# Seven half-size products for batch one, and a new order of the pieces, in an attention and squared-ReLU kernel

## The chip, the core and the metric

The kernel runs on one core of a Trainium2 chip. Five engines run side by side, each through its own queue in order: TensorE (PE, matmuls, with the weight loads shown as PEld), VectorE (DVE), ScalarE (ACT), GpSimd (POOL) and SyncE (SP, which here only issues DMAs). They wait for one another on semaphores. The metric is the time of one execution in device microseconds; the time before is 215.47 us, the median of 3 runs from 215.01 to 215.59.

## What is computed

Two steps, joined. In the first, for each of 8 batches and 8 heads, 512 rows of `x` (64 wide) attend to 32 state rows, and the 32 state rows attend to the 512 rows of `x`:

```python
a = softmax(scale * x @ state.T);   xread = a @ state     # 512 rows
a2 = softmax(scale * state @ x.T);  sread = a2 @ x        # 32 rows
attn_out = concatenate([xread, sread], axis=2)
```

The heads are laid side by side, which gives 8 * 544 = 4352 tokens of width 512. In the second step each token goes through two layers, 512 to 2048 and back to 512:

```python
h = tokens @ w_in
r = maximum(h, 0)
g = s * (r * r) + b
out = g @ w_out
```

## The kernel before

A program writes the instructions from a list of short words, `ORDER` (lines 15 to 78). Each word is one piece of work, its numbers are the batch and the part, and a last letter, where there is one, is the engine: A for ACT, V for DVE, G for POOL. The loop at lines 736 to 739 reads the list from front to back and calls the function of each word from the table `pieces`. Since every engine works through its own queue in order, the list sets, for each engine, the order of its pieces; what is written for different engines runs side by side as far as the semaphores let it.

One batch passes through these pieces.

- Attention of the 512 rows: `x` loads the batch (POOL issues two DMAs; from batch 3 on behind a tiny copy, `ahead`, that waits for the transpose `xT` of the batch before), `xT` transposes it (DVE), `T` makes the scores (PE), `U` transposes them, `mu`, `D`, `E1`, `z`, `At` and `A` are the softmax in between (DVE, E1 on ACT, `D` and `At` on DVE or POOL). `A` is what the first layer multiplies.
- Because the attention is linear in the states, `M` (PE) multiplies the states with `w_in`, 512 columns at a time (four pieces), and `Mc` copies the result from PSUM into f16 (ACT or DVE).
- First layer: `l.b.f` (line 483) multiplies A and M for 128 of the 2048 columns, two matmuls of 512 columns, into `hps`, and ACT takes the ReLU into `r`. `hps` has two PSUM buffers. Batch 0 does part of it in halves of 256 tokens (`lh`). `s` squares two or four such blocks into `g` (`sh` for halves), on ACT or DVE.
- Second layer of batches 0 and 1: `L.b.rr.q` (line 510), four matmuls of 512 columns that sum a quarter of the 2048 for 128 tokens, and `out`, which scales, adds the bias and stores (DVE, then DMAs from SP).
- Second layer of batches 2 to 7: seven products of half-size blocks in place of eight (a Strassen-like scheme). `g` and `w_out` are cut into 2 x 2 blocks. `wsum` makes the sums T1 to T4 of the weight blocks once (eight DVE pieces). `S.b.k.h` makes the four sums of the activation blocks, two halves each (1024 columns a half), mostly in place. `P.b.u` (line 596), u from 0 to 13, is half of one of the seven products: eight matmuls of 256 columns into one of three PSUM tiles, X, Y and W, which share two buffers. `ev` (line 611) scales and adds them into the output tile, seven evictions on DVE, and `put` stores.
- Attention of the 32 state rows: `nm`, `nms`, `E2`, `a2` are the softmax, `tr` transposes by DMA, `xn` loads `x` in another layout (four POOL DMAs; two buffers), `V` (PE, line 408) multiplies, `srd` (ACT) collects. At the end `lsr`, `ssr`, `S_sr`, `P_sr` and `ev_sr` take all 256 of these rows through the two layers.

Three kinds of PE pieces use small tiles of the array, 64 or 128 rows by 32 or 64 columns: `T`, `M` and `V`, and with them `cps` (column sums of `w_out`, for the bias). They write to one of two pairs of PSUM banks, made by `two_banks` (line 133): pair "pt" when `own` is 1, pair "pa" when it is 0. A third number on `M` and `T` chooses; `V` always took "pa". A piece can write to its pair when the piece before it there has been copied out.

POOL's queue carries the loads of `x`, `xn`, `w_in` and `w_out` in the order of the list, and the few pieces marked G in between. SP's queue carries the stores and `tr`.

Of the kernel before, what the change touches and what calls it, by code (L numbers as in the profile page):

```python
# [77 lines left out]
]  # L78


# [1 line left out]
def kernel(  # L82
# [17 lines left out]
    B, H, S, D = x.shape  # L100
# [3 lines left out]
    P = 128  # L104
# [28 lines left out]
    def two_banks(name, dtype=FP32, own=False):  # L133

        pool, tag = (ps_t, "pt") if own else (ps_a, "pa")
        return pool.tile([P, 2, 2048 // mybir.dt.size(dtype)], dtype, name=name, tag=tag)
# [27 lines left out]
    own = konst.tile([P, 2], FP32, name="own")  # L164
# [240 lines left out]
        a2T = sm(b, "a2T", [P, NG * SCH, P], FP16, apool, 2)  # L405
        nc.sync.dma_start_transpose(out=a2T, in_=at[b]["a2"].rearrange("p g s -> p (g s)"))

    def at_V(*bs):

        pair = two_banks(f"vps_{bs[0]}")  # L410
        for v, b in enumerate(bs):
            vps = pair[:, v, : NK * Ns].rearrange("p (k n) -> p k n", n=Ns)
            a2T, xn = at[b]["a2T"], xn_t[b]
            for k in range(NK):
                for g in range(NG):
                    hp = k ^ 2 * g
                    for i in range(SCH):
                        mm(
                            vps[D * g : D * g + D, k, :],
                            xn[:, 4 * g + k, i, :],  # L420
                            a2T[:, SCH * g + i, Ns * hp : Ns * hp + Ns],
                            start=(i == 0),
                            stop=(i == SCH - 1),
                            tp=(0, D * g),
                        )
            at[b]["vps"] = vps
# [343 lines left out]
```

## Time and profile before

The profiled execution took 214.72 us; its span, from the first to the last instruction, is 212.9 us. It ran with a mean granted TensorE clock of 0.989.

| what | us | count |
|---|---|---|
| first layer, matmuls `hps`, busy | 66.1 | 240 |
| second layer of batches 0 and 1, matmuls `ops`, busy | 31.9 | 128 |
| ReLU `r` on ACT, busy | 69.2 | 120 |
| loads `xn` on POOL | 18.6 | 32 |
| chain that ended last: share of PE | 77% | |

"Busy" counts the time in which at least one instruction of the group ran, so overlapping instructions count once. The "mean" of a group is the length of one instruction from start to end; where instructions overlap, the next one starts before that. In a view in order of time a row gives the start, the length of a merged run, the engine, the line, what is written and read, the shape, and how many instructions were merged. In brackets stands the idle time before it and what ended it. Most matmuls of this kernel carry the line of a helper, 140, so they are told apart by the tile that they write: `opf_X`, `opf_Y`, `opf_W` are the products P, `ops` the pieces L, `hps` the pieces l, `mps` the pieces M, `vps` the pieces V, `T_None` the pieces T.

### The profile page before, as it was taken

The numbers are of one execution on the slowest core, as the hardware profiler recorded it, in microseconds if no ns is written. First come the engines' busy times: TensorE is split into PE (matmuls) and PEld (weight loads), VectorE is DVE, ScalarE is ACT, GpSimd is POOL, SyncE is SP. The second block draws the span as 40 slices with busy tenths as digits, with TensorE's granted clock in tenths as the row PEclk, the third lists the DMA queues.
The fourth block names the chain that finished last, engine by engine and source line by source line (L and its number), as shares of the span: only waits on it lengthen the run. The fifth ranks groups of instructions, "written<-read, shape, count | busy, mean of one in ns | idle before, by whom it ended". The sixth has DMA issues, their size and how long they took to land.

```text
span 212.9 us, 4690 instructions
## 1 busy us (share of the span) xinstructions
PE 202.8 (95%) x1891; PEld 126.6 (59%) x1891; DVE 179.5 (84%) x272; ACT 170.9 (80%) x279; POOL 42.8 (20%) x72
## 2 busy tenths in 40 slices
PE   7688999999999999999999999999999999999991
PEld 2224443344444447667777567677675778888881
DVE  2899999999999979899999899989799563766671
ACT  4589988899979899989999989999698998454300
POOL 8554002771202130002404007006200000000000
PEclk9979999999999999999999999999999999999998
DMA  6999999199950939306961881628932640070045
GB/s 148 178 206 207 195 205 166 12 150 226 184 125 4 147 62 161 75 4 129 191 129 22 130 198 17 85 49 150 204 46 49 154 97 3 17 183 0 2 127 173
DMA packets 32107, 24.54 MB, mean 115 GB/s; under 512 B 12884, under 2 KB 25940, under 8 KB 32084
## 3 DMA queue, kind: packets, MB, share of 16 engines
q0 software_dynamic: 16848, 12.52, 41.0%
q1 hardware_dynamic: 13952, 10.75, 21.0%
q10 hardware_dynamic: 1284, 0.95, 1.5%
q8 instruction: 15, 0.25, 0.4%
q14 instruction: 8, 0.07, 0.1%
HBM read 25.72 MB, written 8.91 MB: 163 GB/s over the span
## 4 chain that ended last, share of the span: by engine, by line
PE 77%; DVE 9%; ACT 7%; DMA 3%; issue 1%; SPq 1%; DVEq 0%
PE hps L466 21%; PE opf_X L140 17%; PE ops L515 13%; PE opf_W L140 7%; PE opf_Y L140 4%; PE hps_sr L466 3%; ACT g L474 3%; PE mps L140 3%; DMA out_dram<-osx 3%; PE dps L684 2%; PE ops_sr_X L140 2%; PE T_None L140 2%; DVE Dm L335 1%; DVE g L476 1%; ACT r L470 1%; PE vps L140 1%
## 5 line engine op out<-in xcount | busy, mean ns | idle before, releaser
L470 ACT ACTIVATE r<-hps 128x512 f16<-128x512 f32 x120 | 69.2, 614 | 11.8 <-PE hps L466 11.0
L466 PE MATMUL hps<-A,M 128*128 128x512 f16 x240 | 66.1, 380 | 0.3 <-ACT rh L496 0.2
L140 PEld LDWEIGHTS <-g 128*128 128x128 f16 x576 | 55.9, 98 | 16.7 <-issue 1.5
L474 ACT ACTIVATE g<-r 128x1024 f16<-128x1024 f16 (+1 forms) x36 | 42.8, 1210 | 0.2
L466 PEld LDWEIGHTS <-M 128*128 128x128 f16 x240 | 22.2, 98 | 18.9 <-issue 5.4
L515 PE MATMUL ops<-w_out,g 128*128 128x512 f16 x128 | 31.9, 379 | 0.0
L585 DVE TENSOR_TENSOR g<-g 128x1024 f16<-128x1024 f16 (+1 forms) x34 | 24.3, 715 | 3.2 <-PE opf_Y L140 1.8
L196 POOL DMA_DIRECT2D xn<-in_x_dram x32 | 18.6, 601 | 38.9 <-PE vps L140 37.4
L155 ACT CAST M<-mps 128x1024 f16<-128x1024 f32 x25 | 25.7, 1035 | 0.9 <-PE mps L140 0.9
L140 PE MATMUL opf_X<-w_T,g 128*128 128x256 f16 x192 | 24.6, 273 | 0.2 <-DVE osx L615 0.2
L515 PEld LDWEIGHTS <-g 128*128 128x128 f16 x128 | 12.2, 98 | 15.1 <-DVE Dm L335 0.4
L615 DVE SCALAR_TENSOR_TENSOR osx<-opf_X,sb_bc,bias_bc 128x512 f32<-128x512 f32 x18 | 13.4, 743 | 6.7 <-PE opf_X L140 5.5
L476 DVE TENSOR_TENSOR g<-r 128x1024 f16<-128x1024 f16 (+1 forms) x14 | 11.6, 830 | 3.1 <-ACT r L470 2.9
L140 PE MATMUL mps<-w_in,stT 64*32 64x512 f16 x256 | 12.5, 407 | 1.2 <-DMA w_in<-in_moe_w_in_dram 1.0
L470 ACT ACTIVATE r_sr<-hps_sr 128x256 f16<-128x256 f32 x16 | 6.1, 383 | 9.0 <-PE hps_sr L466 8.7
L140 PE MATMUL opf_Y<-w_out,g 128*128 128x256 f16 x96 | 12.5, 273 | 0.0
L140 PE MATMUL opf_X<-w_out,g 128*128 128x256 f16 x96 | 12.3, 273 | 0.0
L140 PE MATMUL opf_W<-w_out,g 128*128 128x256 f16 x96 | 12.3, 273 | 0.0
L140 PE MATMUL opf_X<-w_T,S 128*128 128x256 f16 x96 | 12.0, 273 | 0.0
L140 PE MATMUL opf_W<-w_T,g 128*128 128x256 f16 x96 | 11.8, 273 | 0.0
L184 POOL COPY ahead<-xT 1x2 f16<-1x2 f16 x5 | 2.5, 507 | 42.6 <-DVE xT L301 42.6
L140 PEld LDWEIGHTS <-S 128*128 128x128 f16 x96 | 9.3, 98 | 2.6 <-issue 0.4
(95 smaller groups left out, 284.0 us busy)
## 6 DMA issues: line engine op xcount, KB each, us to landing
out_dram<-osx SPq DMA_DIRECT2D x44, 128.0 KB, 2.4
xn<-in_x_dram POOLq DMA_DIRECT2D x32, 128.0 KB, 5.1
xh<-in_x_dram POOLq DMA_DIRECT2D x14, 256.0 KB, 4.6
w_in<-in_moe_w_in_dram POOLq DMA_DIRECT2D x8, 256.0 KB, 9.2
w_out<-in_moe_w_out_dram POOLq DMA_DIRECT2D x4, 512.0 KB, 13.9
out_dram<-osb SPq DMA_DIRECT2D x16, 64.0 KB, 5.2
out_dram<-osb SPq DMA_DIRECT2D x8, 128.0 KB, 3.3
xf<-in_x_dram SPq DMA_DIRECT2D x2, 256.0 KB, 3.6
```

The lines of the kernel that those rows point to most:

```text
L140: return nc.tensor.matmul(out, lhsT, rhs, start=start, stop=stop, tile_position=tp, is_transpose=is_transpose, skip_group_check=skip,)
L155: (engine.copy if engine is nc.scalar else engine.tensor_copy)(out, in_)
L184: nc.gpsimd.tensor_copy(ahead, at[b - 1]["xT"][0:1, 0, 0])
L196: nc.gpsimd.dma_start(out=xn_t[b][32 * jh : 32 * jh + 32].rearrange("t h c d -> t h (c d)"), in_=x[b].rearrange("h (t jh c) d -> jh t h (c ...
L466: nc.tensor.matmul(hps, lhsT, rhs, start=(i == 0), stop=(i == len(terms) - 1))
L470: nc.scalar.activation(R_t[tag, q][:, i], hps, AF.Relu)
L474: nc.scalar.activation(g, r, AF.Square)
L476: e.tensor_mul(g, r, r)
L515: nc.tensor.matmul(ops_t[tag, rr], G_t[tag][:, f, P * rr : P * rr + P], w_out_f(f), start=(v == 1 and f == 4 * q), stop=(v == NKF // 4 and ...
L585: e.tensor_tensor(out, x, y, op)
L615: nc.vector.scalar_tensor_tensor(out, fast(b, name[0]), s_bc, out if plus else bias, ALU.mult, ALU.add)
L684: nc.tensor.matmul(dps, ones16[:, :P], ones16, start=True, stop=True)
```

## The change

Three things change in the code. `V` gets a number in front that chooses the PSUM pair. In the list, batch one's second layer is no longer 16 pieces L with four `out`, but 14 pieces P with eight S, seven `ev` and four `put`. And from the word `sb` on the list stands in a new order, in which some pieces also change engine or PSUM pair. In front of `sb` nothing changes.

```diff
-    def at_V(*bs):
+    def at_V(own, *bs):
 
-        pair = two_banks(f"vps_{bs[0]}")
+        pair = two_banks(f"vps_{bs[0]}", own=own)
```

The list past `sb` before (its first part, which has the head, and the part in which batch one's second layer begins):

```diff
-    "lh.0.0.0 sh.0.0.0.V lh.0.6.0 sh.0.6.0.V lh.0.2.1 xT.1.1 sh.0.2.1.V wout.2 sb lh.0.0.1 M.0.2.0 T.1.1 "
-    "U.1 Mc.0.2.A lh.0.4.0 lh.0.4.1 mu.1 D.1.V sh.0.4.0.A l.0.10 keep.1 L.0.1.0 lh.0.6.1 sh.0.6.1.V "
-    "l.0.11 M.1.2.1 l.0.9 M.0.3.0 E1.1 l.0.8 s.0.10.2.V Mc.0.3.V",
...
-    "s.1.8.2.V cps.3 l.1.15 mu.2 c L.0.1.3 L.0.0.3 keep.2 x.3 l.1.7 l.1.12 M.2.1.1 Mc.2.1.A xT.3 "
-    "sh.0.4.1.A bias D.2.G l.1.13 out.0.1 L.0.0.2 T.3.1 nm.3 U.3 E1.2 M.2.2.0 l.1.5 sh.0.0.1.A nms.3.A "
...
-    "s.1.6.2.A L.0.3.0 L.1.0.2 s.1.4.2.A M.3.0.0 M.2.3.1 l.2.0 l.1.14 wsum.T2.0.V L.1.0.1 wsum.T4.0.V "
```

and after:

```diff
+    "lh.0.0.0 sh.0.0.0.V lh.0.6.0 sh.0.6.0.V lh.0.2.1 xT.1.1 sh.0.2.1.V wout.2 sb lh.0.4.0 lh.0.4.1 "
+    "M.0.2.0 sh.0.4.0.V Mc.0.2.A T.1.1 U.1 lh.0.0.1 lh.0.6.1 M.1.2.0 mu.1 sh.0.4.1.G l.0.9 keep.1 l.0.8 "
+    "D.1.V E1.1 L.0.0.0 l.0.11 Mc.1.2.V L.0.1.0 z.1 At.1.V",
+    "M.0.3.1 M.1.3.0 Mc.0.3.A l.0.10 A.1 l.0.12 l.0.15 L.0.0.1 s.0.10.2.V Mc.1.3.A l.0.13 pair.4.16 l.1.9 "
+    "L.0.1.1 turn.4.12.V s.0.12.2.A l.0.14 l.1.15 xT.2 M.2.0.0 l.1.10 l.1.11 wsum.T1.0.V T.2.1 keep.2 "
+    "l.1.8 l.1.1 s.0.8.2.G L.0.0.2 Mc.2.0.V s.0.14.2.V U.2 wsum.T3.0.V l.1.3 wout.3 x.3 xn.2 sh.0.0.1.A "
+    "l.1.0 xn.3 cps.0 cps.2 s.1.8.2.A cps.1 cps.3 M.2.1.1 L.0.1.2 s.1.10.2.A mu.2 L.0.1.3 wsum.T1.1.V "
+    "Mc.2.1.A l.1.7 c l.1.2 D.2.G E1.2 xT.3 bias L.0.0.3 l.1.6 out.0.1 l.1.13 s.1.0.4.V out.0.0 T.3.1 "
+    "M.2.2.0 l.1.12 s.1.6.2.A wsum.T2.0.V L.0.2.3 x.4 l.1.14 l.1.5 sh.0.6.1.A s.1.12.4.A z.2 L.0.2.2 U.3 "
+    "L.0.3.3 Mc.2.2.A L.0.3.2 At.2.G L.0.3.1",
+    "nm.3 nms.3.A E2.3.1 wsum.T3.1.V l.1.4 mu.3 A.2 L.0.2.0 E2.3.0 L.0.2.1 l.2.7 xT.4 out.0.2 l.2.5 "
+    "s.1.4.2.A M.2.3.0 wsum.T2.1.V T.4.1 l.2.8 wsum.T4.1.V l.2.2 L.0.3.0 a2.3 Mc.2.3.A D.3.G l.2.1 "
+    "out.0.3 l.2.10 E1.3 P.1.1 S.1.3.1.V U.4 nm.4 S.1.1.1.G l.2.0 S.1.3.0.G l.2.4 nms.4.A P.1.3 E2.4.0 "
+    "E2.4.1 x.5 turn.12.16.A tr.3 mu.4 P.1.0 l.2.6 l.2.3 P.1.2 M.3.0.1 M.3.1.0 ev.1.X1 s.2.4.2.A "
+    "S.1.2.1.V l.2.13 s.2.6.2.V ev.1.Y S.1.1.0.V P.1.5 Mc.3.1.A s.2.2.2.A P.1.7 S.1.2.0.V l.2.15 "
+    "s.2.0.2.A z.3 P.1.4 l.2.9 At.3.V l.2.11 ev.1.X2 xn.4 Mc.3.0.A D.4.V V.0.3 P.1.6 srd.3 l.2.14 l.2.12 "
+    "A.3 S.1.4.0.V P.1.9 M.4.2.0 M.3.2.1",
...
+    "Mc.6.0.A s.5.2.2.A l.5.6 M.6.1.1 M.6.2.0 s.5.12.2.G l.5.0 P.4.4 E2.0.0 l.5.4 l.5.1 put.3.1.0 P.4.6 "
...
+    "S.5.1.1.V l.6.4 put.4.0.0 S.5.2.0.G s.6.14.2.A ev.5.X1 S.5.2.1.V l.6.9 P.5.5 ev.5.Y P.5.4 l.6.5 "
```

Counted over the whole list, pieces change engine like this: three more `Mc` on ACT and three fewer on DVE; of the squares `s`, eleven instead of fourteen on DVE, 37 instead of 36 on ACT, two on POOL; one half square `sh` from ACT to POOL; on POOL also `D.3`, `S.1.1.1`, `S.1.3.0`, `S.5.2.0`, and `At.2` in place of `At.6`.

93 rows, old and new, of the table ORDER are left out of this document.

## The prediction

> **What bounds the kernel now.** I read the page's totals first, then the busy time by stretches, then the chain of waits, and last the order of time around single steps. The totals and the time slices:
>
> ```profile
> span 212.9 us, 4690 instructions
> PE 202.8 (95%) x1891; PEld 126.6 (59%) x1891; DVE 179.5 (84%) x272; ACT 170.9 (80%) x279; POOL 42.8 (20%) x72
> PE   7688999999999999999999999999999999999991
> ```
>
> TensorE (PE) has no visible hole between the fourth slice (about 21 us) and the last. A busy PE can still run below its peak, so I looked at what full pieces cost in the chain of waits, and at the stretches:
>
> ```profile
> 44.99 2.59 PE ops L515 x12
> 87.46 1.75 PE opf_W L140 x16
> 189.68 0.87 PE opf_Y L140 x8
> ```
>
> ```profile
> 20.00:100.00 80.00, 79.58 (x634) 39.19 (x633) 76.44 (x101) 74.18 (x118) 17.44 (x29) 1.00 0.75 124
> 100.00:120.00 20.00, 19.88 (x257) 14.29 (x256) 18.76 (x28) 19.16 (x31) 4.64 (x8) 1.00 0.72 120
> ```
>
> The columns are the stretch, its length, then busy time of PE, weight loads, VectorE (DVE), ScalarE (ACT), GpSimd (POOL), the granted clock, and DMA. Twelve matmuls of 512 columns pass in 2.59 us, sixteen of 256 columns in 1.75 us, at a granted clock of 1.00: each costs what its columns cost, and pieces of one kind cost the same early and late. So from 20 us on a microsecond of PE work removed is a microsecond saved, as long as nobody is late for PE. The two helpers are nearly full too: between 20 and 100 us DVE is idle for 80 - 76.4 = 3.6 us and ACT for 5.8 us. That is the margin in which this change has to live.
>
> **PE's saving.** A piece L (four matmuls of 512 columns) costs 2.59 / 3 = 0.863 us, a piece P (eight of 256) 1.75 / 2 = 0.874. Batch one gives up 16 L, 13.81 us, and gets 14 P, 12.23 us: 1.58 us saved. The second saving is in the small tiles, the pieces M, T, V and cps:
>
> ```profile
> 38.09 1.03 PE L466 MATMUL hps<-A,M 128*128 128x512 f16 x4
> 39.05 0.41 PE L140 MATMUL mps<-w_in,stT 64*32 64x512 f16 x8
> 39.39 0.39 PE L140 MATMUL bps<-c,ones 128*128 128x512 f16 x1
> 49.67 0.62 PE L140 MATMUL mps<-w_in,stT 64*32 64x512 f16 x16
> 50.23 1.04 PE L466 MATMUL hps<-A,M 128*128 128x512 f16 x4
> ```
>
> Two l pieces cost half of 1.73 us (eight such matmuls), 0.86, yet they take 39.05 - 38.09 = 0.96 before a small piece, which then holds PE for 0.34: a lone M costs 0.44. Two M side by side hold it for 50.23 - 49.67 = 0.56, with the same 0.10 in front 0.66, so the second adds 0.22. Each pair of groups merged saves 0.2 us. In the old order the 51 small pieces stand in 29 groups, in the new one in 26: 0.6 us. PE's floor falls by 1.58 + 0.6 = 2.2 us. The weight loads have room (39 of 80 us busy). Nothing else changes on PE.
>
> **What the other engines get.** Their prices:
>
> ```profile
> L474 ACT ACTIVATE g<-r 128x1024 f16<-128x1024 f16 x30 | 31.2, 1058 | 0.1
> L474 ACT ACTIVATE g<-r 128x2048 f16<-128x2048 f16 x6 | 11.8, 1972 | 0.1
> L474 ACT ACTIVATE g<-rh 128x512 f16<-128x512 f16 x3 | 1.9, 649 | 0.0
> L155 ACT CAST M<-mps 128x1024 f16<-128x1024 f32 x25 | 25.7, 1035 | 0.9 <-PE mps L140 0.9
> L155 DVE CAST M<-mps 128x1024 f16<-128x1024 f32 x7 | 8.5, 1216 | 0.8 <-PE mps L140 0.8
> L585 DVE TENSOR_TENSOR g<-g 128x1024 f16<-128x1024 f16 x32 | 21.9, 683 | 1.4 <-PE opf_X L140 1.0
> L615 DVE SCALAR_TENSOR_TENSOR osx<-opf_X,sb_bc,bias_bc 128x512 f32<-128x512 f32 x18 | 13.4, 743 | 6.7 <-PE opf_X L140 5.5
> L525 DVE SCALAR_TENSOR_TENSOR osb<-ops,sb_bc,bias_bc 128x512 f32<-128x512 f32 x8 | 5.9, 734 | 0.0
> L335 POOL TENSOR_TENSOR Dm<-U,mu 128x1024 f32<-128x1024 f32 x1 | 1.9, 1908 | 4.9 <-DVE mu L331 4.9
> L356 POOL TENSOR_TENSOR At<-E,rz 128x1024 f16<-128x1024 f16 x1 | 1.9, 1909 | 11.9 <-DVE rz L347 11.9
> ```
>
> DVE over the whole kernel: six sums S of batch one at 0.68 and seven evictions at 0.74 come (+9.3); four stores at 0.73, three casts Mc at 1.22, D.3 (priced as a cast) and S.5.2.0 go (-8.5); its squares become two fewer of the two-wide and one fewer of the four-wide kind (-2.6, a square taken as a sum of its width). Net -1.8 us. ACT: three casts at 1.03, one four-wide square at 1.97, one half square of 0.65 fewer: +4.4 us. POOL gets six more whole operations at 1.9 (D.3, S.1.1.1, S.1.3.0, S.5.2.0, s.0.8.2, s.5.12.2), one half (sh.0.4.1, about 1.0), and trades At.6 for At.2: +12.4 us, in a queue that idles 80%. No row shows POOL squaring or adding f16 sums; the two rows of POOL arithmetic are 1.91 for f32 and f16 alike, so I take 1.9; the bounds are DVE's 0.68 for the same sum and 2.6, should it wait out one such sum first.
>
> What matters is where it falls. Up to the first product of batch three (about 99 us), counting list against list, ACT has one cast more, one two-wide and one four-wide square more, one half square less: +1.03 + 1.04 + 1.97 - 0.65 = +3.4 us. The stretch gets shorter by most of PE's saving, say 1.8. ACT's idle time there falls from 5.8 to 5.8 - 3.4 - 1.8 = 0.6 us: ACT becomes as full as PE. DVE's load there falls by about 1.3, its idle time ends near 3.6 + 1.3 - 1.8 = 3.1.
>
> One ACT wait I can name. E1.2 now stands behind D.2 on POOL, and D.2 behind ten loads (x.3, xn.2, xn.3) where it had only x.3:
>
> ```profile
> 32.16 0.55 POOL L184 COPY ahead<-xT 1x2 f16<-1x2 f16 x1 [10.83 <-DVE xT L301]
> 38.61 1.91 POOL L335 TENSOR_TENSOR Dm<-U,mu 128x1024 f32<-128x1024 f32 x1 [4.87 <-DVE mu L331]
> 40.85 1.11 POOL L187 DMA_DIRECT2D xh<-in_x_dram  x2 [0.20 <-issue]
> 46.80 0.58 POOL L196 DMA_DIRECT2D xn<-in_x_dram  x1 [0.78 <-DMA xh<-in_x_dram]
> 41.59 1.08 ACT L341 ACTIVATE E<-Dm 128x1024 f16<-128x1024 f32 x1
> ```
>
> Ten such loads in one go took from 40.85 to 47.38, 6.5 us. Started when x.3 starts now, or up to 1 us earlier because xT.2 moves up, they end at 38.2 to 39.2, and D.2 at 40.1 to 41.1 instead of 40.52. ACT, however, comes to E1.2 sooner: the same 18 first-layer, 7 L and 4 half pieces stand in front of it that PE has done by 39.05 (row above), so with the last relu about 39.6, where it now comes at 41.59. Behind E1.2 queue the relus of l.1.6 and l.1.13, and PE has two PSUM buffers for them; then it waits. ACT's forced idle is 0.5 to 1.5 us.
>
> wout.3, the last quarter of w_out, is moved behind a POOL square whose relus come from the first l pieces, so to about 26 us instead of 20.58:
>
> ```profile
> 20.58 0.75 POOL L210 DMA_DIRECT2D w_out<-in_moe_w_out_dram  x1 [1.79 <-DMA w_out<-in_moe_w_out_dram]
> DMA to landing us min/median/max: 11.2/13.9/14.6
> xh<-in_x_dram POOLq DMA_DIRECT2D x14, 256.0 KB, 4.6
> ```
>
> cps.2, cps.3 and the first L of that quarter need it near 36 us. With 13.9 it would land at 39.9 and PE lose up to 4; with twice the 4.6 us of a load of half its size that meets a shorter queue, at 35.2, and nothing is lost. The landing times grow from 11.2 to 14.6 us because each waits for the loads ahead; after 21.3 POOL issues none until 32.16, so a later issue mostly finds the queue shorter. I take nothing, near the second row. The early xn loads follow it and are needed only by V, far later.
>
> The sums of the weights (T1 to T4) move ahead of batch one's products and number eight as before. The V pieces may take either PSUM pair: no instruction is added. The tail (the last sums and stores) has the same pieces; nothing there, since PE's last products cover the sums; if one came late, its 0.7 would be the price.
>
> **The loss.** Bounds on what ACT's fullness costs PE: at the low end nothing; at the high end all of the 5.8 us idle stays, because it was waiting for data, and PE loses 5.8 - 0.6 = 5.2. The nearest row is the stretch from 100 to 120, with ACT 96% busy, in which one PE wait stands:
>
> ```profile
> 119.47 0.41 PE L140 MATMUL mps<-w_in,stT 64*32 64x512 f16 x8
> 120.05 0.41 PE L140 MATMUL mps<-w_in,stT 64*32 64x512 f16 x8 [0.17 <-ACT M L155]
> ```
>
> 0.58 instead of 0.22: 0.36 us in 20, or 1.4 in 80. I take half of that, 0.7, which is also the lower half of the E1.2 wait, because the rest of ACT's idle time is time in which it was ahead of PE.
>
> Sum: -2.2 + 0.7 = -1.5 us. The profiled execution, 214.72 us with 212.9 of span, would become 213.2. It lies 0.75 under the median of the runs shown (215.47), so for the median I say 215.47 - 1.5 = 214.0.
>
> **Rivals.** *ACT becomes the bound* (the slower side). Place: ACT's queue from the head to batch three. If 4 of its 5.8 us idle are true waits, PE loses 4 - 0.6 = 3.4 and the time is 215.47 - 2.2 + 3.4 = 216.7. It decides from 3.5 us of idle that stays (loss 2.9, gain gone). For it: every square moved to ACT. Against it stands the largest of ACT's waits, for PE's hps (view of waits: total, times, longest): there ACT was ahead of PE.
>
> ```profile
> ACT r L470 <- PE hps L466: 11.0, 23, 1.0
> ```
>
> *A draw*: 1.6 to 2.8 us lost, about 215.2. *All of it arrives*, or the head's waits shrink too: 213.3 and below; the lists part at sb, 17.4 us, where PE still waits.
>
> *DVE and POOL hold each other up.* Beside today's two POOL operations DVE ran none with two SBUF tensors:
>
> ```profile
> 129.04 1.91 POOL L356 TENSOR_TENSOR At<-E,rz 128x1024 f16<-128x1024 f16 x1 [11.86 <-DVE rz L347]
> 129.37 1.24 DVE L327 STREAM_TRANSPOSE U<-T_None 128x1024 f32<-128x1024 f32 x1
> 131.16 0.68 DVE L585 TENSOR_TENSOR g<-g 128x1024 f16<-128x1024 f16 x1
> ```
>
> So its trace cannot say whether a sum on DVE would have waited. With seven more, each can hold a DVE sum for up to its 1.9 us. The new order puts transposes, reductions and evictions beside most of them (U.4, nm.4, mu.4 and an eviction, 4.4 us, beside the two sums of batch one, 3.8), but ev.5.X1 alone, 0.74, stands beside S.5.2.0, so a wait of 1.2 is in sight there. If half of all 12.4 us block DVE, 6.2 less the 3.1 idle: 3.1 lost, 215.47 - 1.5 + 3.1 = 217.1. The Trainium skill (SBUF — State Buffer, Who interferes with whom) states just this: a DVE instruction with two SBUF inputs and a GpSimd one that reads SBUF exclude each other for a whole instruction. No run here shows it yet.
>
> *It does not do what it says*: the products of batch one could wait for the weight sums. All of T1 to T4 stand in the list ahead of the product that reads them, so I give that nothing.
>
> **Chances.** Forecast 0.42 (faster); all of it arrives 0.16 (faster); draw 0.20; ACT the bound 0.14; DVE and POOL 0.08. Faster 0.58, same 0.20, slower 0.22, where 0.3%, 0.65 us, is what a measurement here can tell from no change. The forecast's own range is 213.3 to 214.8. For 8 in 10 it must take in the draw and the nearer part of the slower cases: 212.8 to 216.7.
>
> **What would show it.** Right: x112 more opf matmuls, 64 fewer ops; PE's last piece about 1.5 us earlier; ACT busy about 77 of the first 78 us after 20; E1.2 waiting for Dm on POOL about 1 us. ACT the bound: PE waits with ACT as releaser between 40 and 90 us. DVE and POOL: sums on DVE longer than 0.68 while POOL computes, or POOL rows longer than 1.9. Wrong altogether: PE waits named for osx, S or x loads in batch one's products.

## The result, and the profile after

The changed kernel takes 213.65 us, the median of 9 runs (212.66 to 214.59), against 215.59 us (215.01 to 216.5, 9 runs) before: a ratio of 0.9907, 95% interval 0.9881 to 0.9934. A second set of runs gave 0.9923 (0.9895 to 0.995). The profiled execution took 212.66 us, 2.06 less than the one before. Its page:

```profile
span 210.9 us, 4809 instructions
PE 200.8 (95%) x1939; PEld 131.3 (62%) x1939; DVE 178.0 (84%) x273; ACT 175.2 (83%) x282; POOL 56.1 (27%) x79
PE 66%; ACT 16%; DVE 10%; DMA 3%; issue 1%; SPq 1%; DVEq 0%
L517 PE MATMUL ops<-w_out,g 128*128 128x512 f16 x64 | 15.6, 379 | 0.0
```

PE has 48 instructions more (112 more of the products, 64 fewer of `ops`), as announced, and is busy 2.0 us less. The third line is the chain of waits: it runs 16% of the span through ACT, where it was 7%. The last rows of the chain before and after, which hold PE's last piece:

```profile
207.58 0.89 PE ops_sr_X L140 x8
```

```profile
205.89 0.89 PE ops_sr_X L142 x8
```

PE's last piece comes 1.69 us earlier. Of the 1.97 us by which the span is shorter, the other 0.28 lies behind this piece, in the last eviction and store. The busy time by stretches, columns as before:

```profile
20.00:100.00 80.00, 79.39 (x732) 44.63 (x730) 78.31 (x105) 78.41 (x123) 29.92 (x38) 1.00 0.73 123
100.00:120.00 20.00, 19.59 (x214) 13.98 (x212) 19.26 (x30) 19.14 (x31) 0.71 (x2) 1.00 0.59 121
```

ACT, the fourth busy time, is now idle for 1.6 of 80 us and DVE, the third, for 1.7, while PE still loses only 0.6. The chain from the first of these rows to the last:

```profile
42.80 0.60 ACT r L472
...
70.94 1.83 ACT M L157 x2
72.81 0.37 PE mps L142
```

Between them every piece of the chain is one of ACT's, although PE has no hole there before the last row. Both are full, and the tracing back takes ACT. This is the state that the prediction called "as full as PE".

To see where PE lost time I priced every piece of its list with the prediction's prices (0.863 an L, 0.874 a P, 0.43 an l, 0.22 an M or cps and 0.22 more for each group of small pieces; T and V at what they take in the trace), summed from `sb` on, and compared each piece's start with this sum. What a piece is late by is what PE has waited so far. The sum falls by 2.2 us, as forecast, and the waits grow by 0.5. A new one of 0.57 stands at the piece P.3.5, a product of batch three; the rest about cancels (0.25 for one of ACT's casts at 72.8 us is new, 0.26 at 120 us and 0.22 at P.5.5 are gone). The order of time around it:

```profile
103.44 0.75 DVE L617 SCALAR_TENSOR_TENSOR osx<-opf_X,sb_bc,bias_bc 128x512 f32<-128x512 f32 x1 [0.56 <-DMA out_dram<-osx]
104.25 1.03 PE L142 MATMUL opf_X<-w_T,g 128*128 128x256 f16 x8 [0.41 <-DVE osx L617]
```

and the chain of waits that leads to it:

```profile
95.11 0.67 DVE osx L617
...
97.05 0.59 SPq L626
...
97.68 5.64 DMA out_dram<-osx
...
103.44 0.76 DVE osx L617
...
104.25 1.03 PE opf_X L142 x8
```

The last eviction of batch two into its first output tile, ev.2.W2, ends at 95.77. SP then issues eight stores one after the other, 0.6 us each, the four of this tile first; the chain follows the fourth, issued at 97.68, whose transfer ends at 103.32. This tile (key 0) holds the first half of the batch's rows, with all columns; the expectations below that call it the tile of columns 0 mean the same one. It has one buffer, so batch three's first eviction, ev.3.X1, waits 0.56 us for the store, and P.3.5, which adds to the PSUM tile that this eviction reads, waits for it. In the kernel before, the same eviction stood at 104.71 and waited for nothing:

```profile
95.18 0.74 DVE L615 SCALAR_TENSOR_TENSOR osx<-opf_W,sb_bc,osx 128x512 f32<-128x512 f32 x1
...
104.71 0.71 DVE L615 SCALAR_TENSOR_TENSOR osx<-opf_X,sb_bc,bias_bc 128x512 f32<-128x512 f32 x1
```

There it was 9.5 us from the start of the one to the start of the other. In the new order it would have been 7.9 (95.03 to 102.88, where DVE began to wait), and the way through the store takes 8.4 (95.03 to 103.44).

The shorter distance alone would not have met the store. Before, the four stores of this tile landed 2.3 to 2.4 us after their issue, the fourth 5.0 us after the start of ev.2.W2; now they take 5.1 to 5.7. What differs beside them is POOL's load `x.7`, two transfers of 256 KB: it is now issued just ahead of the stores, where before it came when the first of them had landed. The rows before, in order of time, with the stores issued between 94 and 101 us (KB each, us to landing):

```profile
95.95 7.85 SPq L624 DMA_DIRECT2D out_dram<-osx  x8
98.76 1.05 POOL L187 DMA_DIRECT2D xh<-in_x_dram  x2 [0.31 <-issue]
...
out_dram<-osx SPq DMA_DIRECT2D x4, 128.0 KB, 2.3
```

and after:

```profile
95.10 1.06 POOL L189 DMA_DIRECT2D xh<-in_x_dram  x2
95.80 5.17 SPq L626 DMA_DIRECT2D out_dram<-osx  x8
```

That the load lengthens the stores is read from the traces side by side (before, the batch's later stores, issued at 101.9 to 103.2 beside POOL's loads, took 4.9 to 5.4 us too). No run moves the load alone.

### The profile page after: what moved, and what is told of

It is laid out like the page before. It is cut to its first block, busy times and chain, and to the rows that moved or that the text cites. A ratio compares the mean times of both kernels' runs of the same rounds, so it can differ in the third digit from the quotient of the medians.

```text
span 210.9 us, 4809 instructions
## 1 busy us (share of the span) xinstructions
PE 200.8 (95%) x1939; PEld 131.3 (62%) x1939; DVE 178.0 (84%) x273; ACT 175.2 (83%) x282; POOL 56.1 (27%) x79
## 4 chain that ended last, share of the span: by engine, by line
PE 66%; ACT 16%; DVE 10%; DMA 3%; issue 1%; SPq 1%; DVEq 0%
PE opf_X L142 18%; PE hps L468 17%; PE opf_W L142 8%; ACT r L472 6%; ACT g L476 4%; PE opf_Y L142 4%; PE hps_sr L468 3%; ACT M L157 3%; DMA out_dram<-osx 3%; PE mps L142 3%; PE dps L686 3%; PE ops L517 3%; DVE osx L617 2%; PE ops_sr_X L142 2%; PE vps L142 2%
## 5 line engine op out<-in xcount | busy, mean ns | idle before, releaser
L142 PEld LDWEIGHTS <-g 128*128 128x128 f16 x672 | 65.3, 98 | 19.0 <-issue 1.7
L476 ACT ACTIVATE g<-r 128x1024 f16<-128x1024 f16 (+1 forms) x37 | 46.3, 1260 | 0.1
L157 ACT CAST M<-mps 128x1024 f16<-128x1024 f32 x28 | 28.3, 1023 | 0.6 <-PE mps L142 0.5
L142 PE MATMUL opf_X<-w_T,g 128*128 128x256 f16 x224 | 28.4, 273 | 0.4 <-DVE osx L617 0.4
L587 DVE TENSOR_TENSOR g<-g 128x1024 f16<-128x1024 f16 (+1 forms) x38 | 27.7, 729 | 1.2 <-PE opf_Y L142 0.5
L617 DVE SCALAR_TENSOR_TENSOR osx<-opf_X,sb_bc,bias_bc 128x512 f32<-128x512 f32 x21 | 15.6, 745 | 3.3 <-PE opf_X L142 1.7
L517 PE MATMUL ops<-w_out,g 128*128 128x512 f16 x64 | 15.6, 379 | 0.0
L478 DVE TENSOR_TENSOR g<-r 128x1024 f16<-128x1024 f16 (+1 forms) x11 | 9.1, 829 | 6.1 <-ACT r L472 6.1
L142 PE MATMUL opf_W<-w_T,g 128*128 128x256 f16 x112 | 14.2, 273 | 0.0
L478 POOL TENSOR_TENSOR g<-r 128x1024 f16<-128x1024 f16 x2 | 3.8, 1892 | 27.7 <-ACT r L472 27.7
L517 PEld LDWEIGHTS <-g 128*128 128x128 f16 x64 | 6.2, 98 | 7.6 <-issue 0.2
```

What stands on the lines that cost most here:

```text
L142: return nc.tensor.matmul(out, lhsT, rhs, start=start, stop=stop, tile_position=tp, is_transpose=is_transpose, skip_group_check=skip,)
L157: (engine.copy if engine is nc.scalar else engine.tensor_copy)(out, in_)
L476: nc.scalar.activation(g, r, AF.Square)
L478: e.tensor_mul(g, r, r)
L517: nc.tensor.matmul(ops_t[tag, rr], G_t[tag][:, f, P * rr : P * rr + P], w_out_f(f), start=(v == 1 and f == 4 * q), stop=(v == NKF // 4 and ...
L587: e.tensor_tensor(out, x, y, op)
```

## The experiments

Theory A: PE's list got 2.2 us shorter, as priced, and 0.5 came back at one new place, the single buffer of the output tile. Theory B, the prediction's own: what came back was taken by ACT's fullness. Rivals for the gain: that it is the order past the head, and not the products and the pairs of small pieces, that saves; and that the work given to POOL does. All edits are to the changed kernel unless said otherwise; words of `ORDER` are shown. Each list is set in fewer lines, so line numbers in these profiles are a few lower. The head, up to `sb`, is edited in none of them, yet `sb` starts anywhere from 17.16 to 17.77 us in these profiles; the last column leaves it out.

| run | ratio to before, 95% interval | PE's last piece starts, us | the same, counted from `sb` |
|---|---|---|---|
| before | 1 | 207.58 | 190.17 |
| the change | 0.9907 (0.9881 to 0.9934) | 205.89 | 188.45 |
| after_again | 0.9923 (0.9895 to 0.995) | 205.86 | 188.56 |
| pairs_split | 0.9954 (0.9932 to 0.9976) | 207.19 | 189.80 |
| prod_undone | 0.9957 (0.9935 to 0.9979) | 207.18 | 189.73 |
| osx_two | 0.9854 (0.982 to 0.9888) | 205.14 | 187.98 |
| osx_two_split | 0.9957 (0.9933 to 0.998) | 206.93 | 189.57 |
| osx_two_prod_undone | 0.9939 (0.9917 to 0.9961) | 207.45 | 189.85 |
| osx_two_old | 1.007 (1.0048 to 1.0092) | 209.27 | 191.91 |
| osx_two_s520 | 0.986 (0.9821 to 0.9899) | 205.20 | 188.02 |
| act_more | 1.0001 (0.9976 to 1.0026) | 208.40 | 191.02 |
| act_more_old | 1.0025 (0.9996 to 1.0054) | 209.42 | 191.66 |
| pool_off | 1.0159 (1.0096 to 1.0222) | 210.33 | 192.79 |
| sum_beside_pool | one run, 214.4 us | 207.65 | 190.22 |

**after_again** is the changed kernel once more, on the chip of the next three.

> The changed kernel once more, as the mark for the other three. Every theory expects its result again: a ratio of about 0.991 to the kernel before, the last PE piece near 206.8 us of the span, one PE wait of about 0.4 us for osx near 104 us.

PE's last piece came within 0.03 us of the first profile, and the wait was there again (0.63 us at the eviction). It belongs to the kernel and not to one execution.

**pairs_split** pulls ten pairs of neighbouring small pieces apart, by moving one of the pair behind the next l or P piece:

```diff
-M.0.3.1 M.1.3.0 Mc.0.3.A l.0.10
+M.0.3.1 Mc.0.3.A l.0.10 M.1.3.0
...
-M.4.1.1 E1.4 M.4.3.0 S.2.2.0.V s.3.0.4.A nm.2 P.2.3
+M.4.1.1 E1.4 S.2.2.0.V s.3.0.4.A nm.2 P.2.3 M.4.3.0
```

> The changed kernel with ten pairs of small-tile pieces pulled apart: the second piece stands one PE piece later. Same instructions, same engines. Theory (each merge of groups saves 0.2 us of PE time and PE has no slack): the last PE piece comes 10 x 0.2 = 2.0 us later than in the changed kernel, the ratio goes to 1.000. Rival (between 42 and 73 us the chain runs through ACT, so a PE switch there is free): five of the ten cost nothing, 1.0 us later, ratio 0.996.

**prod_undone** puts batch one's second layer back into 16 pieces L with four `out`, at the places of the products:

```diff
-P.1.1 S.1.3.1.V ... P.1.3 ... P.1.0 ... P.1.2 ... ev.1.X1
+L.1.0.0 ... L.1.0.1 ... L.1.0.2 ... L.1.0.3 ... out.1.0
```

> The changed kernel with the second layer of batch one put back to 16 pieces L and four stores in the places of the products; its eight sums, seven evictions and the four puts are gone. Theory (products are worth their PE columns, 1.58 us, and the helpers keep up): 1.6 us later than the changed kernel, ratio 0.998. Rival (ACT and DVE are the bound around batch one, so the sums and evictions that go pay back what PE loses): 0.5 us later or less, ratio 0.993 or lower.

Both came out between their two theories: PE's last piece 1.3 us later, where PE's list had grown by 2.0 and by 1.58. In both, the wait at P.3.5 is gone; the eviction behind it no longer waits for the store (its row in prod_undone, in order of time):

```profile
104.53 0.75 DVE L611 SCALAR_TENSOR_TENSOR osx<-opf_X,sb_bc,bias_bc 128x512 f32<-128x512 f32 x1
```

So each edit gets back a part of what it costs: in prod_undone PE is 1.75 us later at P.2.0 (78.40 against 76.65) and 1.16 later at P.3.4, behind the eviction. It is not PE's lateness that takes the wait away. In sum_beside_pool (below) ev.2.W2 starts at 96.78, in prod_undone at 96.76, and there the next batch's eviction does wait, as it does in act_more (0.81) and pool_off (0.61), with PE 2.3 and 3.7 us later:

```profile
105.21 0.75 DVE L612 SCALAR_TENSOR_TENSOR osx<-opf_X,sb_bc,bias_bc 128x512 f32<-128x512 f32 x1 [0.58 <-DMA out_dram<-osx]
```

What differs is the fourth store: it lands at 104.28 in prod_undone and at 105.09 in sum_beside_pool, though it is issued at 99.4 in both. In pairs_split it also lands sooner, 7.7 us after the start of ev.2.W2 instead of 8.3, and the eviction comes 8.2 us after it instead of 7.9. Why the store lands sooner there was not found. A direct test had to take the wait away.

**osx_two** gives the output tile of key 0 a second buffer, and pays for the space with two of the four buffers of `osb`, which only batch zero and the state rows use now:

```diff
-opool = ctx.enter_context(tc.tile_pool(name="opool", bufs=4))
+opool = ctx.enter_context(tc.tile_pool(name="opool", bufs=2))
...
-tag=f"osx{key}", bufs=1)
+tag=f"osx{key}", bufs=2 if key == "0" else 1)
```

> The changed kernel with two buffers for the output tile osx of the first row half (and two instead of four for osb, which makes the room). Theory (the 0.56 us for which the eviction X1 of batch three waits for batch two's store is a true loss): the PE wait near 104 us is gone, the last PE piece comes 0.5 us sooner, ratio 0.989. Rival (another wait takes its place, ACT being as full as PE there): no change, ratio 0.991; a second rival, that the two osb buffers now hold up a store of batch zero: later than the changed kernel.

The eviction goes ahead at 102.49 with no wait, 7.8 us after ev.2.W2. PE's last piece comes 0.74 us earlier; 0.28 of that is the head, so the buffer is worth 0.47. The ratio is 0.9854: a faster kernel than both, 212.07 us, with an interval that does not touch the one of after_again on the same chip. In its view of waits PE has none for `osx` any more; past the head one row is left:

```profile
PE hps L463 <- ACT M L152: 0.4, 1, 0.4
```

(columns: engine and line that waited, for whom, us in total, times, longest; the other rows of PE's waits all belong to the head). Theory A stands for this part. The remaining question is whether the two savings are whole once the wait is gone.

**osx_two_split**: osx_two with the ten pairs pulled apart.

> The kernel after with two buffers for the output tile of columns 0 (as osx_two) and the ten pairs of small pieces pulled apart (as pairs_split). Theory (the pairs are worth their whole 2.0 us of PE's order, and pairs_split showed only 1.3 because a later PE no longer met the wait for the output tile): with that wait gone, PE's last piece 1.8 to 2.2 us later than in osx_two, ratio to before about 0.995. Rival (the pairs are worth 1.3 us, some of the pulled-apart pieces fill time in which PE would wait anyway): 1.2 to 1.5 later, ratio about 0.991 to 0.992.

**osx_two_prod_undone**: osx_two with batch one back in L pieces.

> The kernel after with two buffers for the output tile of columns 0 and batch one's second layer back in 16 pieces of 512 columns. Theory (seven products are worth their whole 1.58 us on PE; the run without the buffer showed 1.3): PE's last piece 1.5 to 1.8 us later than in osx_two, ratio to before about 0.993. Rival (what they save, the fuller ACT and DVE take part of): at most 1.1 later, ratio 0.991 or less.

Counted from `sb`, the pairs cost 1.59 us now, where they cost 1.35 without the second buffer. That lies between what theory A (1.8 to 2.2) and the rival (1.2 to 1.5) expected, and piece by piece there is something of both. The first pair, at 24 us, costs nothing, since PE waits there for one of ACT's casts in any case (0.40 us in osx_two, 0.56 here): that is the rival's mechanism. The nine others cost 0.2 each, and 0.3 of it comes back later: 0.1 is osx_two's wait for ACT's cast at 72.5 us, which a later PE doesn't meet; where the rest comes from was not looked for. The ratios within this set of runs (0.9957 against 0.986 of osx_two_s520) give 2.1 us, with intervals that leave about 1 us either way.

Undoing the products costs 2.31 us, above what either expected. Of it 0.56 is no part of the edit: PE was already that much later at 26 us (piece l.0.12 starts at 26.24 instead of 25.68), ahead of the first piece that differs. The 1.75 that are left are what prod_undone showed at P.2.0, and near the 1.58 priced; the ratios (0.9939 against 0.986) give 1.7. (That `osb` has two buffers does no harm there: no `out` waits for a store.) So the price of the products holds, and so does that of a pair where PE does not wait anyway. With 1.58 for the products and 0.6 for three groups they make up the whole 2.2 us, so a gain of the order as such is not needed to account for it; no run puts the products into the old order. The two runs without the second buffer had hidden 0.46 us of the products' cost and 0.24 of the pairs'.

**osx_two_old**: the kernel before, with the same two lines changed.

> The kernel before with two buffers for the output tile of columns 0. Theory (there only 0.2 us of PE's waits are for that tile, at the fifth product of batch five): PE's last piece 0.1 to 0.4 us earlier, ratio 0.998 to 1.000. Rival (the second buffer is worth about the same 0.7 us or more in any order, and osx_two says nothing about the change): ratio 0.996 or less.

A miss, and the fault is in the experiment. In the kernel before, batch one also uses `osb`, and with two buffers its first `out` waits for a store of batch zero (order of time):

```profile
49.61 0.75 DVE L521 SCALAR_TENSOR_TENSOR osb<-ops,sb_bc,bias_bc 128x512 f32<-128x512 f32 x1 [2.09 <-DMA out_dram<-osb]
...
50.41 1.02 PE L511 MATMUL ops<-w_out,g 128*128 128x512 f16 x4 [1.61 <-DVE osb L521]
```

PE loses 1.6 us there, so the run doesn't tell what the second buffer alone is worth in the kernel before; that stays open. It does show the same kind of wait from the other side: a store that has not landed stops DVE, and 0.8 us later PE. And it shows that the space became free only through the change, which took batch one off `osb`.

**act_more** loads ACT with 3.0 us more: a four-wide square (1.91 in this trace) and a two-wide one (about 1.0) go from DVE to ACT.

```diff
-s.1.0.4.V
+s.1.0.4.A
...
-s.2.4.2.A S.1.2.1.V l.2.13 s.2.6.2.V
+s.2.4.2.A s.2.6.2.A S.1.2.1.V l.2.13
```

> The changed kernel with two squares moved from DVE to ACT between 40 and 62 us: s.1.0 (four wide, 1.97 us) and s.2.6 (two wide, 1.04 us). Theory (ACT is as full as PE there, and its chain carries that stretch): PE falls behind by most of the 3.0 us; less the 0.6 us of the osx wait near 104 us that a later PE no longer meets, the last PE piece comes 1.5 to 2.4 us later, ratio 0.998 to 1.003. Rival (ACT still has room in its waits for PE): less than 0.5 us, ratio 0.993 or lower.

**act_more_old** does the same in the kernel before (s.1.0.4 and s.2.2.2).

> The same edit in the kernel before: s.1.0 (four wide) and s.2.2 (two wide) from DVE to ACT, the same 3.0 us. Theory (there ACT still idled 5.8 us between 20 and 100 us): PE loses less than 0.7 us, ratio 1.003 or lower. Rival (ACT's waits were true waits already then): 2 us or more, ratio 1.009 or higher.

The changed kernel loses its whole gain: ratio 1.0001, PE's last piece 2.51 us later, 2.27 of it by P.3.0. The store's wait, which I had expected to go away, grew by 0.25 (0.81 instead of 0.56 at the eviction). Two of PE's new waits are for ACT, the first right behind the added four-wide square, the second 3 us behind the other (order of time):

```profile
44.89 0.59 PE L463 MATMUL hps<-A,M 128*128 128x512 f16 x2 [0.87 <-ACT r L467]
...
66.47 0.59 PE L463 MATMUL hps<-A,M 128*128 128x512 f16 x2 [0.84 <-ACT r L467]
```

The kernel before takes the same load with almost no loss in that stretch. By the sum of pieces PE loses 0.35 us there, at one place (39.8 us). Its last piece is nonetheless 1.84 us later: 0.46 of that stands in the head, ahead of the edit, and the most elsewhere. (The profiled run, 217.18 us, is the slowest of its ten; their median is 215.92, against 215.35 for the kernel before.) The eviction ev.5.X1 met the store of its tile, and P.5.5 waited 1.28 us for it, where before 0.2 was lost.

```profile
152.64 1.03 PE L136 MATMUL opf_X<-w_T,g 128*128 128x256 f16 x8 [1.28 <-DVE osx L611]
```

So the change left ACT a margin of about 0.7 us at these places (3.0 in, 2.3 out by P.3.0), where the kernel before had more than 2.5; but the change itself did not go over the edge.

**pool_off** takes seven of the operations that the change gave to POOL back to DVE (s.0.8.2, D.3, S.1.1.1, S.1.3.0, S.5.2.0) and ACT (sh.0.4.1, s.5.12.2).

```diff
-s.0.8.2.G ... D.3.G ... S.1.1.1.G l.2.0 S.1.3.0.G
+s.0.8.2.V ... D.3.V ... S.1.1.1.V l.2.0 S.1.3.0.V
```

> The changed kernel with the seven new POOL operations taken back: S.1.1.1, S.1.3.0, S.5.2.0, s.0.8.2 and D.3 on DVE, sh.0.4.1 and s.5.12.2 on ACT (At.2 stays on POOL). DVE gets 3.3 us more before 60 us, where it had 1.7 us idle from 20 to 100. Theory (DVE and ACT are at their limit without POOL): PE loses 1 to 2 us on the way to batch two's products, ratio 0.995 to 1.000. Rival (POOL's operations held DVE up about as much as they relieved it): within 0.5 us of the changed kernel, ratio 0.990 to 0.993.

The loss is larger than expected: ratio 1.0159, PE's last piece 4.44 us later. Of it 1.95 stands at one place that my edit made: the square s.0.8.2, now in DVE's queue behind a weight sum, holds its `r`, ACT waits for the buffer, and PE for ACT.

```profile
33.28 1.08 ACT L467 ACTIVATE r<-hps 128x512 f16<-128x512 f32 x2 [1.91 <-DVE g L473]
...
33.92 0.59 PE L463 MATMUL hps<-A,M 128*128 128x512 f16 x2 [1.88 <-ACT r L467]
...
64.13 1.05 PE L137 MATMUL opf_X<-w_T,g 128*128 128x256 f16 x8 [0.52 <-DVE g L582]
```

Another 1.5 us (four waits between 62 and 66 us, the last row one of them) are batch one's products waiting for their sums, which is the mechanism I meant. How much of 4.4 a better placing would save was not tried. What follows is only that, in this list, POOL's work is needed: without it DVE is late for batch one.

**sum_beside_pool** moves the weight sum T4.0, a DVE sum of two SBUF tensors, beside POOL's sums S.1.1.1 and S.1.3.0.

```diff
-U.4 nm.4 S.1.1.1.G
+U.4 wsum.T4.0.V nm.4 S.1.1.1.G
```

> The changed kernel with the weight sum T4.0 (DVE, two inputs in SBUF, 0.68 us) moved between the transpose U.4 and the maximum nm.4, that is into the time of the POOL sum S.1.1.1. Theory (two-input sums on DVE and POOL arithmetic shut each other out): T4.0 lasts until the POOL sum ends or POOL's sum is longer, so one of them is 0.5 us or more above 0.68 or 2.12. Rival (no such exclusion, and the long rows of 0.94 and 1.30 us were something else): T4.0 takes 0.68 us and the POOL sum 2.12.

```profile
55.21 2.12 POOL L582 TENSOR_TENSOR g<-g 128x1024 f16<-128x1024 f16 x1 [4.10 <-DVE S L582]
...
56.15 1.74 DVE L552 TENSOR_TENSOR w_T<-w_out,w_T 128x1024 f16<-128x1024 f16 x1
...
57.29 2.58 POOL L582 TENSOR_TENSOR S<-g 128x1024 f16<-128x1024 f16 x1
57.81 1.21 DVE L375 TENSOR_REDUCE nm<-T_None 128x2 f32<-128x1024 f32 x1
...
60.79 0.41 PE L137 MATMUL mps<-w_in,stT 64*32 64x512 f16 x8 [0.92 <-ACT E L386]
```

The DVE sum takes 1.74 us instead of 0.68. It ends at 57.89, which is 0.56 after POOL's sum (57.33). POOL's next sum then takes 2.58 instead of 2.12: it waits out the rest of DVE's. The reduction nm.4 behind it comes late, ACT's softmax after it, and PE loses 0.92. PE's last piece is 1.76 us later in all. Not all of this is the hold: the sum's own 0.68 us now also stand ahead of nm.4, and no run tells the two apart.

**osx_two_s520** puts S.5.2.0 back from POOL to DVE in osx_two.

> osx_two with the sum S.5.2.0 back on DVE. Theory: the sum beside it on DVE falls from 1.30 to 0.68 us, so DVE does two sums in the time of the one it did before, and PE's last piece moves by less than 0.2 us: ratio to before within 0.0015 of osx_two. Rival (the DVE sum held by POOL delays the batch's products): 0.4 us or more earlier than osx_two.

No difference in the time: 205.20 against 205.14, ratio 0.986 against 0.9854. In osx_two the sum beside POOL's is held longer than in the changed kernel, 2.11 us in place of 1.30; the first two rows are osx_two, the third is the same DVE sum here:

```profile
144.92 2.13 POOL L582 TENSOR_TENSOR g<-g 128x1024 f16<-128x1024 f16 x1 [13.85 <-DVE g L582]
145.49 2.11 DVE L582 TENSOR_TENSOR g<-g 128x1024 f16<-128x1024 f16 x1
...
146.15 0.68 DVE L582 TENSOR_TENSOR g<-g 128x1024 f16<-128x1024 f16 x1
```

With the other sum on POOL, DVE is done at 147.60, with both sums to do at 146.83. So the piece on POOL saves DVE nothing here, and being held for 1.4 us costs PE nothing.

## Why the prediction came out as it did

**PE's saving, 2.2 us: right, and shown.** The sum of PE's pieces falls by 2.2 us. Pulling ten pairs apart costs 2.0 in the sum and 1.59 measured, 0.2 for each pair at which PE does not wait anyway, the price used for the three groups fewer; undoing the products costs 1.75, where 1.58 was priced. That a microsecond off PE's list is a microsecond off the time was right only up to the store of batch two, whose landing depends on more than PE.

**The loss, 0.7 us: right in size (0.5) by luck, wrong in place.** The failing step is "I take half of that, 0.7", which puts the loss on ACT's fullness. ACT became as full as said: 78.4 of 80 us, 98%, against 77 of 78 forecast. But past the head PE waits for ACT hardly more than before. The row behind the 0.7 was also misread: the first of two M pieces holds PE for about 0.33, as the prediction's own lone M shows (0.34), and not for the 0.22 that a second one adds, so the wait at 120 us was about 0.25 and not 0.36. The loss lay at P.3.5. A wait for osx stood in the prediction only as a sign of being "wrong altogether", and for batch one's products rather than batch three's. To find it, each eviction's new time has to be set against the landing of the store that frees its tile, and not with the old landing: 9.5 us between the two evictions became 7.9, which is still more than the 5.0 that the store's way took before. One must also see that `x.7` now runs beside these stores, which take 5.1 to 5.7 us there and not 2.4.

**ACT's idle time.** The argument against the slower rival was that ACT's largest wait, 11.0 us for PE's `hps`, is time in which ACT was ahead. After:

```profile
ACT r L472 <- PE hps L468: 5.4, 14, 0.9
```

This wait halved and PE lost nothing by it, so the argument holds, and rival one (216.7) did not come. How near it was, act_more shows: 3.0 us more, and the time is that of the kernel before. DVE's idle time was forecast too high: 1.7 of 80 us are left, not 3.1. Which part of that count was off was not looked for.

**E1.2 behind D.2: about 1 us forecast, 0.14 found.** In order of time:

```profile
38.62 1.93 POOL L337 TENSOR_TENSOR Dm<-U,mu 128x1024 f32<-128x1024 f32 x1
...
39.34 1.10 ACT L472 ACTIVATE r<-hps 128x512 f16<-128x512 f32 x2
...
40.58 1.06 ACT L343 ACTIVATE E<-Dm 128x1024 f16<-128x1024 f32 x1
```

D.2 ended at 40.55, inside the 40.1 to 41.1 that I gave. The relu before E1.2 ended at 40.44, not 39.6: I had priced what PE had done by then, and not when ACT itself would be through: its relu ended only 0.1 us before D.2 did.

**POOL's prices: 1.9 was right for squares and too low for sums.** By shape:

```profile
L587 POOL TENSOR_TENSOR g<-g 128x1024 f16<-128x1024 f16 x2 | 4.3, 2126 | 17.9 <-DVE g L587 13.8 <-ACT r L472 4.0
L478 POOL TENSOR_TENSOR g<-r 128x1024 f16<-128x1024 f16 x2 | 3.8, 1892 | 27.7 <-ACT r L472 27.7
L587 POOL TENSOR_TENSOR S<-g 128x1024 f16<-128x1024 f16 x1 | 2.1, 2123 | 0.0
```

POOL is busy for 27% of the span, and in front of the two sums of batch one it had waited 4.0 us for its data; that the 0.2 costs no time was not tested.

**DVE and POOL hold each other up: the mechanism is real, the price was not paid.** At the named place the wait in sight, 1.2, came out at 0.62 (1.30 instead of 0.68):

```profile
145.66 2.13 POOL L587 TENSOR_TENSOR g<-g 128x1024 f16<-128x1024 f16 x1 [13.85 <-DVE g L587]
...
147.04 1.30 DVE L587 TENSOR_TENSOR g<-g 128x1024 f16<-128x1024 f16 x1
```

One more sum, at 58.94, takes 0.94. The other operations on POOL stand beside transposes, reductions and evictions, as the prediction read from the list, and those keep their usual lengths. osx_two_s520 shows that at the named place even 1.4 us of it costs no time, sum_beside_pool that a badly placed sum can cost up to 1.76. In all of these the DVE sum ends about 0.55 us after POOL's, whenever it began. The Trainium skill (SBUF — State Buffer, Who interferes with whom) says that the port pair which the two engines share is an exclusive lock, that a DVE instruction with two SBUF inputs contends for it with a GpSimd one that reads SBUF, and that the order of issue decides who is blocked. The 1.74 and 2.58 of sum_beside_pool agree, DVE waiting for POOL and then POOL for DVE.

**wout.3: nothing, right, by 0.4 us.** It was issued at 25.5 us and landed 9.5 us later, at 35.0, no later than in the kernel before (35.2, issued at 20.58). The first `cps` ran at 35.41 without a wait for it:

```profile
35.41 1.05 PE L142 MATMUL cps<-w_out,ones 128*32 128x512 f16 x16
```

**The sums of the weights** do not all stand ahead of batch one's products, as the prediction says: `wsum.T4.0` stands between them, but ahead of P.1.13 and P.1.12, which read T4. PE does not wait for them.

**The tail: nothing was forecast, 0.28 us were gained** behind PE's last piece. What shortened it was not tried.

## What to carry to other kernels

A saving on a full engine is worth its length only up to the first wait that the new list brings; after shortening or reordering a list, set each store's landing against the time at which its buffer is next written, and take the landing with the loads that will then run beside it (2.4 us became 5.1 to 5.7 here). An experiment that undoes a part can hide its worth behind the same wait, so repeat it with the wait removed: the products and the pairs measured 1.3 us each in one kernel and 1.75 and 1.59 in the other. Compare two profiles from the same piece on: here up to 0.6 us of a difference lay in a head that nobody had edited. When two engines are equally full, the chain of waits may pass through either; a deliberate overload of one (3.0 us in, 2.3 us out) tells how much margin is left.

## What was not expected of the hardware

- On POOL a sum of two different tensors of 128x1024 f16 takes 2.12 us, a square of one tensor 1.89 (rows above).
- The eight stores of batch two landed 5.7 us after their issue (median), where the median of all 52 is 2.4. They shared the DMA engines with POOL's loads of x, whose queue took 69% of these engines between 95 and 104 us (DMA view of this stretch: queue, packets, MB, share; then issues, KB each, us to landing):

```profile
q0 software_dynamic: 855, 0.80, 69.4%
...
out_dram<-osx SPq DMA_DIRECT2D x8, 128.0 KB, 5.7
```

- On ACT a long row need not be a slow one. The two relus of 128x512 at 67.04 take 1.47 us where a pair takes 1.1, but they start 0.23 us after the small cast of `srdT` does, while its row still runs. From the cast's end at 67.60 to their own at 68.51 it is 0.91 us, about what two relus add to the chain elsewhere (0.98 at 44.35).

```profile
66.81 0.79 ACT L431 CAST srdT<-vps 128x128 f16<-128x128 f32 x1
67.04 1.47 ACT L472 ACTIVATE r<-hps 128x512 f16<-128x512 f32 x2
```
